# Transposing q on VectorE in 32x32 blocks instead of on TensorE, in a linear-attention and SwiGLU kernel

## The chip, the cores and the metric

The kernel runs on one core of a Trainium2 chip. A core has five engines with a queue of instructions each: TensorE (PE: matrix products out of SBUF into PSUM), VectorE (DVE), ScalarE (ACT), GpSimd (POOL) and SyncE (SP), which in this kernel issues nearly all DMAs. [...] The metric is the time of one execution on the device in microseconds, as a median over several runs.

## The reference

Linear attention without softmax, a norm for each head, and a gated feed-forward layer on the result. Everything is float32.

```python
# q, k, v: (8 batches, 8 heads, 576 tokens, 64)
kv  = np.einsum('bhsd,bhse->bhde', k, v)             # 64x64 per head and batch
out = np.einsum('bhsd,bhde->bhse', q, kv)
rms = np.sqrt(np.mean(out * out, axis=-1, keepdims=True) + 1e-06)
x   = (out / rms * g_norm)                           # -> 4608 tokens x 512
g   = x @ w_gate                                     # 512 x 1536
y   = (g * (1 / (1 + np.exp(-g)))) * (x @ w_val)     # silu(g) * val
return y @ w_out                                     # 1536 x 512
```

## The kernel before

**Blocks.** The 4608 tokens are worked off in nine blocks (n = 0 to 8) of 512. A batch has 576 tokens, so a block begins in one batch and ends in the next; `parts` (class `Att`) says which rows of which batch a tile of 128 tokens has. In each block `Att` makes x, and `Ffn` makes the feed-forward layer in an **up** stage (x times the gate and value weights, result h) and a **down** stage (h times `w_out`). The products are in Strassen-Winograd form: seven products, P1 to P7, for a 2x2 split, twice nested in the up stage from block 2 on (class `Inner`, 12 units per block, line 580). The down stage (class `Down`, line 431) takes them in the order 1, 5, 6, 7, 2, 4, 3. The weights that the nested form needs are combinations, made once and kept in DRAM; `Stream` brings them back in 51 chunks per block through the buffers `t` (nine of them, line 659). The three products P5, P7 and P4 of the down stage need combinations of `w_out` that GpSimd makes into three of the same buffers each (`turn_t`, line 111 in the profile, "T for P5", and so on).

**Attention is woven in one block ahead.** While block n is in its up stage, k and v of block n+1 are loaded (line 223) and multiplied (`kv`, line 255) in two steps, after a third and two thirds of the stage. q of block n+1 is loaded after the second (`load_q`, line 238): 128 tokens in the partitions, all 8 heads in the columns, in pieces of 64 floats. Between up and down, `turn` transposes q on TensorE against an identity matrix (line 272, 16 transposes of 128x128 in a block), into PSUM, and ScalarE copies them into `qt` (line 274). Then, in the down stage: after P1 half 0 of q is multiplied with kv (`product`, line 292), squared (ScalarE, line 303), summed (VectorE, line 304), turned into 1/rms by three Newton steps on small tiles (`root`, lines 310 to 322), and scaled (`scale`, line 330); after P6 the scaled half is transposed on TensorE (`turn_x`, line 339), and half 1 goes the same way; after P2 its `turn_x` follows, and `sums` makes the combinations of x that the next up stage needs.

**Buffers.** `ld` has four buffers (k and v of a pair of heads take one each, q takes two), `r` has five for every intermediate of 128x2048 floats, qt among them. PSUM is split into pools: a (1), b (3), c (2), m (2).

**What sets the order.** The order of instructions on each engine isn't simply that of the program. The framework's planner plays the program through on a model: each engine takes the earliest-written instruction among those that are ready and whose buffer is free, so an instruction that is ready early can be queued ahead of ones written before it. `add_manual_dep` and `issue_after` add an order by hand. Once planned, each engine works its queue strictly in order. All loads, weights included, share SyncE's queue.

The lines that matter:

```python
                for j in range(NS):
                    nc.tensor.transpose(ps[:, j], self.q[t][:, j], ident)
                if t % 2 or self.n == 1 or self.n > DEEP:
                    nc.scalar.copy(out=self.qt[:, t], in_=ps)
...
        if nxt:
            nxt.turn()
        if n + 2 < NB:
            blocks[n + 2].load_kv((0, 1))
        ffn.down(nxt.steps() if nxt else [])
```

Of the kernel before, what the change touches and what calls it, by code (L numbers as in the profile page):

```python
# [8 lines left out]
F32 = mybir.dt.float32  # L9
# [5 lines left out]
P = 128  # L15
# [3 lines left out]
def kernel(  # L19
# [41 lines left out]
    nc = tc.nc  # L61

    B, H, S, D = q.shape
    NT, DM = out.shape
    FF = moe_w_gate.shape[1]
    T = 4
    BLK = P * T
# [3 lines left out]
    NS = DM // P  # L71
# [7 lines left out]
    def pool(name, bufs, **kw):  # L79
        return ctx.enter_context(tc.tile_pool(name=name, bufs=bufs, **kw))  # L80

    consts = pool("consts", 1)
    ld_pool = pool("ld", 4)
# [30 lines left out]
    def ring():  # L114

        return r_pool.tile([P, 4, BLK], F32, name="r")
# [67 lines left out]
    class Att:  # L184
# [29 lines left out]
        def load_kv(self, js):  # L214
            if self.n == B:
                return
            for j in js:
                hs = slice(2 * j, 2 * j + 2)
                for i, (tiles, src) in enumerate(((self.k, k), (self.v, v))):
# [6 lines left out]
                        )  # L226
                    tiles.append(t.rearrange("p h (t d) -> p h t d", t=KT))

        def load_q(self, i):
            if self.n == 1:  # L230
                tiles = [t_tile().rearrange("p a b -> p (a b)") for _ in range(2)]
            else:
                ld = ld_pool.tile([P, 2 * BLK], F32, name="ld")
                tiles = [ld[:, 0:BLK], ld[:, BLK : 2 * BLK]]
            for t in range(2):
                tile_ = tiles[t].rearrange("p (h d) -> p h d", h=H)
                for b, s0, p0, p1 in self.parts(2 * i + t):
                    nc.sync.dma_start(
                        out=tile_[p0:p1], in_=q[b, :, s0 : s0 + p1 - p0, :].rearrange("h p d -> p h d")
                    )  # L240
                self.q.append(tile_.rearrange("p (j u) d -> p j (u d)", u=2))
# [22 lines left out]
        def turn_q(self, i, pools=None):  # L264

            if i == 0:
                self.qt = ring().rearrange("p t (j c) -> p t j c", j=NS)
            for t in (2 * i, 2 * i + 1):
                pool = pools[t % 2] if pools else m_psum
                ps = pool.tile([P, NS, P], F32, name=pool.name[0])  # L270
# [4 lines that stand above are left out]
                else:  # L275
                    nc.vector.tensor_copy(out=self.qt[:, t], in_=ps)
# [67 lines left out]
        def sums(self):  # L344
# [5 lines left out]
            sub(nc.vector, s4, a12, a21)  # L350
            if self.n >= DEEP:
                self.xi = x_pool.tile([P, 3, 7, P], F32, name="xi")
# [53 lines left out]
    XI = {5: 0, 7: 1, 3: 2}  # L406

    DEEP = 2

    class Quad:  # L410

# [41 lines left out]
    class Up(Quad):  # L453
# [41 lines left out]
        def multiply(self, p):  # L495
            super().multiply(p)
            ffn = self.ffn
            if ffn.n != DEEP - 1:
                return
# [136 lines left out]
    class Stream:  # L636
# [10 lines left out]
        def enable(self, n):  # L647
            if DEEP <= n < NB:
                self.next += [(n, d, c) for d in range(NP // 2) for c in range(len(CHUNKS))]
                self.pump()  # L650
# [23 lines left out]
    def t_tile(key=None):  # L674

        stream.held.append(key)
        return t_pool.tile([P, 2, 2 * P], F32, name="t")
# [128 lines left out]
    class Ffn:  # L806
# [22 lines left out]
        def up(self, fill):  # L829
# [3 lines left out]
            for d in range(NP // 2):  # L833
                if self.n < DEEP:
                    units += [Up(self, 2 * d), Up(self, 2 * d + 1)]
# [17 lines left out]
                if unit is None:  # L853
                    last.multiply(p)

        def down(self, fill):
            down = self.down_
            fill = dict(zip((1, 6, 2), fill))
            for p in (1, 5, 6, 7, 2, 4, 3):
                if p == 1:  # L860
                    down.turn_t(7, self.ended)
                if p == 6:
                    down.turn_t(4)
                down.multiply(p)
                self.make(12)
                if p in fill:
                    fill[p]()
                if p == 1:
                    down.turn_s3()
# [31 lines left out]
    def weights(upto):  # L901
        nonlocal loaded, rounded
        while rounded < min(upto, len(pieces)):
            while loaded < min(rounded + 4, len(pieces)):
                load_w(*pieces[loaded])
                loaded += 1
            round_w(*pieces[rounded])
            rounded += 1

    def t2(place, b22, b11):  # L910

        sub(nc.vector, place, b22, place)
        add(nc.vector, place, place, b11)

    blocks = [Att(n) for n in range(NB)]
# [7 lines left out]
    for n in range(NB):  # L923
        ffn = Ffn(n, blocks[n])
        nxt = blocks[n + 1] if n + 1 < NB else None
        if n == 0:

            with tc.issue_after(scaled.ins):
                weights(2)
            ffn.plain_up(0, (0,))  # L930
            scaled = blocks[0].second()
            for f in range(NF):
                with tc.issue_after(scaled.ins):
                    weights(2 * (f + 2))
                if f == 1:
                    ffn.plain_up(1, (0,))
                    ffn.plain_up(0, (1,))
                ffn.plain_up(f, (1,)) if f == 1 else ffn.plain_up(f) if f else None
            weights(len(pieces))
            pairs = wo.rearrange("p (j e) d -> p e j d", e=2)  # L940
            t2(pairs[:, 0, :, HD:DM], pairs[:, 1, :, HD:DM], pairs[:, 0, :, 0:HD])
            nxt.room = x_pool.tile([P, 3, 7, P], F32, name="xi").rearrange("p a b c -> p (a b c)")
            nxt.load_kv(range(NS))
            for i in range(2):
                nxt.load_q(i)
            ffn.plain_end()
            nxt.kv(range(NS))
        else:

            def third():  # L950
                nxt.kv((0, 1))
                nxt.load_kv((2, 3))

            def two_thirds():
                nxt.kv((2, 3))
                for i in range(2):
                    nxt.load_q(i)

            ffn.up({4: third, 8: two_thirds} if nxt else {})
        if nxt:  # L960
            nxt.turn()
        if n + 2 < NB:
            blocks[n + 2].load_kv((0, 1))
        ffn.down(nxt.steps() if nxt else [])
        if n == 0:

            with tc.issue_after(nxt.halves[0].ins):
                for j in range(NP):
                    t2(wv[j][:, 0:2], wv[j][:, 2:4], wg[j][:, 0:2])
# [31 lines left out]
```

## Time and profile before

| | |
|---|---|
| time, median of 3 runs | 1065.49 us (1065.43 to 1066.24) |
| span of the profiled execution | 1063.9 us |
| TensorE busy | 1036.4 us, 97% |
| VectorE, ScalarE, GpSimd busy | 701.6, 245.0, 365.9 us |
| granted TensorE clock | 0.988 of full speed on average, 1.00 in blocks 3 to 8 |
| DMA | 161.87 MB, 50.4% of the DMA engines' span |
| start of the down stage of blocks 3 to 7 | 473.41, 585.17, 696.93, 808.69, 917.43 us |

The rows of the profile begin with the line of the kernel, the engine and the operation, then what is written and what is read. In rows of a timeline the start and the length come first, in us; square brackets give the time for which the engine sat idle before it, and what ended that. Rows of the chain of waits give start, length and the work that then set the time. The row over a stretch gives, after its limits and length, the busy time of PE, PE's weight loads, DVE, ACT and POOL with the number of instructions, the granted clock, the share of the DMA engines and GB/s. The blocks from 2 to 7 repeat with a period of 111.76 us (block 7 is shorter since block 8 begins no new batch, and so has no k and v of its own).

### The profile page before, as it was taken

The page shows a single profiled execution, that of the slowest core. Times are in us where ns is not written, and L with a number is a line of the kernel's source. Part 1 is how long each engine was busy: PE and PEld are TensorE (multiplying, and loading weights), DVE is VectorE, ACT ScalarE, POOL GpSimd, SP SyncE. Part 2 cuts the span into 40 slices and gives each one's busy share as a digit, 9 for nine tenths or more (in the row PEclk, how much of TensorE's full clock was granted, in tenths as well). Part 3 has the DMA queues.
Part 4 walks back from the last instruction along what each step waited for, and adds up shares of the span by engine and source line. Part 5 has one row for each costly group of instructions (what it writes and reads, how often), then busy time and mean ns, then how long its engine had stood idle before and what let it go on. Part 6 is the DMA issues. An engine that isn't in the chain of part 4 may idle for free.

```text
span 1063.9 us, 21805 instructions
## 1 busy us (share of the span) xinstructions
PE 1036.4 (97%) x8780; PEld 934.8 (88%) x8780; DVE 701.6 (66%) x1245; ACT 245.0 (23%) x392; POOL 365.9 (34%) x280
## 2 busy tenths in 40 slices
PE   4899999988999999999999999999999999999998
PEld 4644688877899989998999899989999899989997
DVE  2999596778656765576666666666567566765661
ACT  2665111221221211222112211221112221211210
POOL 0000453344025701462156305640456026602670
PEclk8899999998999999999999999999999999999999
DMA  8787103565569326741576237713783265125611
GB/s 235 225 272 224 59 4 107 166 169 159 166 208 254 99 72 193 237 150 61 163 241 174 82 127 226 226 53 129 215 236 77 80 205 194 53 81 188 199 36 40
DMA packets 154644, 161.87 MB, mean 152 GB/s; under 512 B 48432, under 2 KB 105648, under 8 KB 154544
## 3 DMA queue, kind: packets, MB, share of 16 engines
q1 hardware_dynamic: 154480, 160.48, 50.4%
q8 instruction: 70, 1.15, 0.5%
q14 instruction: 30, 0.25, 0.1%
q0 software_dynamic: 64, 0.00, 0.0%
HBM read 138.02 MB, written 22.41 MB: 151 GB/s over the span
## 4 chain that ended last, share of the span: by engine, by line
PE 93%; DVE 3%; SPq 2%; DMA 1%; POOL 1%; issue 0%; ACT 0%; DVEq 0%; POOLq 0%
PE b L580 25%; PE b L431 20%; PE c L580 12%; PE c L431 10%; PE a L580 6%; PE a L431 5%; PE b L882 4%; PE c L882 4%; PE m L255 2%; PE m L339 2%; PE m L292 1%; SPq L223 1%; PE b L292 1%; DMA ld<-in_moe_w_gate_dram 1%; PE b L272 1%; PE m L272 1%
## 5 line engine op out<-in xcount | busy, mean ns | idle before, releaser
L110 POOL TENSOR_TENSOR r<-r 128x256 f32<-128x256 f32 (+1 forms) x105 | 110.3, 1056 | 363.0 <-DVE r L110 357.8
L110 DVE TENSOR_TENSOR r<-b,r 128x512 f32<-128x512 f32 (+1 forms) x273 | 162.2, 607 | 61.3 <-PE b L580 56.6
L110 DVE TENSOR_TENSOR r<-c,r 128x512 f32<-128x512 f32 (+1 forms) x179 | 109.1, 620 | 99.0 <-PE c L580 56.0
L111 POOL TENSOR_TENSOR t<-wo 128x512 f32<-128x512 f32 x81 | 112.7, 1417 | 164.7 <-DVE wo L110 109.0
L580 PE MATMUL b<-x,t 128*128 128x128 f32 x1092 | 151.2, 276 | 0.0
L580 PEld LDWEIGHTS b<-x,t 128*128 128x128 f32 x1092 | 136.0, 192 | 0.6
L110 DVE TENSOR_TENSOR r<-a,r 128x512 f32<-128x512 f32 (+1 forms) x99 | 62.6, 632 | 83.2 <-PE a L580 53.1
L112 POOL TENSOR_TENSOR h<-r 128x1024 f32<-128x1024 f32 (+1 forms) x40 | 81.5, 2054 | 93.2 <-DVE r L110 79.7
L580 PE MATMUL c<-xi,t 128*128 128x128 f32 x840 | 112.1, 275 | 0.0
L580 PEld LDWEIGHTS c<-xi,t 128*128 128x128 f32 x840 | 102.8, 192 | 0.0
L431 PE MATMUL b<-t,h 128*128 128x256 f32 x432 | 97.1, 381 | 0.0
L431 PE MATMUL b<-wo,h 128*128 128x256 f32 x432 | 96.2, 379 | 0.0
L431 PEld LDWEIGHTS b<-wo,h 128*128 128x128 f32 x432 | 81.4, 190 | 10.7
L431 PEld LDWEIGHTS b<-t,h 128*128 128x128 f32 x432 | 80.7, 190 | 11.1 <-issue 0.2
L594 ACT COPY r<-b 128x512 f32<-128x512 f32 x63 | 36.9, 586 | 219.1 <-PE b L580 191.7
L580 PE MATMUL b<-xi,t 128*128 128x128 f32 x588 | 79.7, 276 | 0.0
L580 PEld LDWEIGHTS b<-xi,t 128*128 128x128 f32 x588 | 72.4, 192 | 0.0
L580 PE MATMUL b<-x,wg 128*128 128x128 f32 x336 | 53.0, 280 | 0.0
L580 PE MATMUL b<-x,wv 128*128 128x128 f32 x336 | 51.2, 275 | 0.0
L431 PE MATMUL c<-t,s 128*128 128x256 f32 x216 | 48.9, 383 | 0.0
L431 PE MATMUL a<-wo,h 128*128 128x256 f32 x216 | 48.3, 379 | 0.0
L431 PE MATMUL c<-wo,h 128*128 128x256 f32 x216 | 48.1, 379 | 0.0
(129 smaller groups left out, 1646.2 us busy)
## 6 DMA issues: line engine op xcount, KB each, us to landing
t<-w SPq DMA_DIRECT2D x336, 256.0 KB, 2.9
out_dram<-r SPq DMA_DIRECT2D x17, 512.0 KB, 2.9
ld<-in_q_dram SPq DMA_DIRECT2D x29, 256.0 KB, 4.6
ld<-in_moe_w_gate_dram SPq DMA_DIRECT2D x12, 512.0 KB, 5.2
ld<-in_moe_w_val_dram SPq DMA_DIRECT2D x12, 512.0 KB, 5.2
ld<-in_moe_w_out_dram SPq DMA_DIRECT2D x12, 512.0 KB, 4.5
w<-t SPq DMA_DIRECT2D x36, 128.0 KB, 2.1
ld<-in_k_dram SPq DMA_DIRECT2D x26, 160.0 KB, 3.1
```

The source lines that it names most:

```text
L110: add = lambda e, o, a, b: e.tensor_tensor(out=o, in0=a, in1=b, op=OP.add)
L111: sub = lambda e, o, a, b: e.tensor_tensor(out=o, in0=a, in1=b, op=OP.subtract)
L112: mul = lambda e, o, a, b: e.tensor_tensor(out=o, in0=a, in1=b, op=OP.mult)
L223: nc.sync.dma_start(out=t[r * D : (r + 1) * D, :, 0 : m * D], in_=src[self.n, hs, s0 : s0 + m * D].rearrange("h (p t) d -> p h (t d)", t=m),)
L255: nc.tensor.matmul(self.kv_ps[r][u * D : (u + 1) * D, j, :], lhsT=self.k[j][rows, u, c, :], rhs=self.v[j][rows, u, c, :], start=(c == 0), ...
L272: nc.tensor.transpose(ps[:, j], self.q[t][:, j], ident)
L292: nc.tensor.matmul(self.ps[i][u][p : p + D, t, j, :], lhsT=self.qt[rows, 2 * i + t, j, p : p + D], rhs=kvs[b % 3][rows, j, :], start=True, ...
L339: nc.tensor.transpose(ps[:, e, t], xt[:, t, j + e], ident)
L431: nc.tensor.matmul(banks[e][:, e], lhsT=lhsT, rhs=rhs, start=first and i == 0 and (e == 0 or banks[0] is not banks[1]), stop=i == self.ste ...
L580: nc.tensor.matmul(ps[:, i, f], lhsT=self.weight(o, p, f), rhs=self.operand(o, p), start=first and (i, f) == (0, 0), stop=True, skip_group ...
L594: nc.scalar.copy(out=dst, in_=ps)
L882: nc.tensor.matmul(t, lhsT=w[f // 2][:, i, P * (f % 2) : P * (f % 2 + 1)], rhs=x[:, i, of], start=(i == 0), stop=(i == NS - 1),)
```

## The change

For the blocks from 4 on (`TURNED`), q is no longer transposed on TensorE. VectorE has a transpose within 32x32 blocks only. To make the whole transpose out of it, the load puts each 32-column quarter of a pair of heads (two heads of 64 columns) into its own 32 partitions, with the tokens in groups of 32 along the columns (`load_quarters`); transposing the 32x32 blocks in place then gives columns in the partitions and tokens along the free dimension, which is what `product` needs. A load of q is thus split into 16 DMAs for four heads (8 where all tokens are of one batch), with pieces of 32 floats, and one VectorE instruction of 128x1024 turns four heads. `qt` is laid out by pair of heads and then by token tile, so that the output of the transpose is contiguous.

So that the loads are there in time, q of block n+2 is loaded at the start of the down stage of block n, a whole block earlier; to keep within the four `ld` buffers, k and v go in four steps of one pair each, after units 2, 5, 8 and 11 of the up stage, each followed by the load of the next pair. T for P4 on GpSimd is made to wait for the scaling of half 0.

```diff
+        def load_quarters(self, i):
+            ld = ld_pool.tile([P, 2 * BLK], F32, name="ld")
+            to = ld.rearrange("p (j g d) -> p j g d", j=2, d=P // 4)
+            cut = 2 * self.n
+            spans = [(self.n - 1, S - D * self.n, 0, cut), (self.n, 0, cut, BLK // 32)]
+            for j in range(2):
+                for r in range(4):
+                    h, d = divmod(r, 2)
+                    for b, s0, g0, g1 in spans:
+                        if g1 > g0:
+                            nc.sync.dma_start(
+                                out=to[32 * r : 32 * (r + 1), j, g0:g1],
+                                in_=q[b, 4 * i + 2 * j + h, s0 : s0 + 32 * (g1 - g0), 32 * d : 32 * (d + 1)].rearrange(
+                                    "(g p) d -> p g d", p=32
+                                ),
+                            )
+            self.q.append(ld)
...
             if i == 0:
-                self.qt = ring().rearrange("p t (j c) -> p t j c", j=NS)
+                self.qt = ring().rearrange("p j (t c) -> p t j c", t=T)
+            if self.n >= TURNED:
+                to = self.qt[:, :, 2 * i : 2 * i + 2].rearrange("p t j c -> p j t c")
+                nc.vector.transpose(out=to.rearrange("p j t c -> p (j t c)"), in_=self.q[i])
+                return
...
                 if p == 6:
-                    down.turn_t(4)
+                    down.turn_t(4, nxt.halves[0] if nxt and nxt.n >= TURNED else None)
...
-            ffn.up({4: third, 8: two_thirds} if nxt else {})
+            def pair(j):
+                nxt.kv((j,))
+                if j + 1 < NS:
+                    nxt.load_kv((j + 1,))
+
+            if not nxt:
+                steps = {}
+            elif n + 1 < TURNED:
+                steps = {4: third, 8: two_thirds}
+            else:
+                steps = {3 * j + 2: lambda j=j: pair(j) for j in range(NS)}
+            ffn.up(steps)
         if nxt:
             nxt.turn()
         if n + 2 < NB:
-            blocks[n + 2].load_kv((0, 1))
-        ffn.down(nxt.steps() if nxt else [])
+            if n + 2 < TURNED:
+                blocks[n + 2].load_kv((0, 1))
+            else:
+                blocks[n + 2].load_kv((0,))
+                for i in range(2):
+                    blocks[n + 2].load_q(i)
+        ffn.down(nxt)
```

More of the change, by code (lines that the diff above doesn't have):

```diff
@@ L227, in load_kv @@
                     tiles.append(t.rearrange("p h (t d) -> p h t d", t=KT))
+        def load_quarters(self, i):
[15 more added lines that the diff above has]
+            self.q.append(ld)
         def load_q(self, i):
+            if self.n >= TURNED:
+                self.load_quarters(i)
+                return
             if self.n == 1:
@@ L266, in turn_q @@
             if i == 0:
-                self.qt = ring().rearrange("p t (j c) -> p t j c", j=NS)
+                self.qt = ring().rearrange("p j (t c) -> p t j c", t=T)
+            if self.n >= TURNED:
+                to = self.qt[:, :, 2 * i : 2 * i + 2].rearrange("p t j c -> p j t c")
+                nc.vector.transpose(out=to.rearrange("p j t c -> p (j t c)"), in_=self.q[i])
+                return
             for t in (2 * i, 2 * i + 1):
@@ L408 @@
     DEEP = 2
+    TURNED = 4
     class Quad:
@@ L854, in up, with down @@
                     last.multiply(p)
-        def down(self, fill):
+        def down(self, nxt):
             down = self.down_
-            fill = dict(zip((1, 6, 2), fill))
+            fill = dict(zip((1, 6, 2), nxt.steps() if nxt else ()))
             for p in (1, 5, 6, 7, 2, 4, 3):
```

## Prediction

> **What bounds the kernel now.** I read the page's busy table first, then the busy time over one block of tokens, then the chain of waits across the end of that block's up stage, and last VectorE's and SyncE's own order of time there. The first two show what the time is made of: TensorE is busy for 97% of the whole span and for all 111.80 us of the block from 473.2 to 585.0 us, at the full granted clock (the 1.00 behind the counts), while VectorE has 40 us to spare, ScalarE 89 us, and the DMA engines half their time. The waits listed for TensorE between 360 and 1020 us are none.
>
> ```profile
> PE 1036.4 (97%) x8780; PEld 934.8 (88%) x8780; DVE 701.6 (66%) x1245; ACT 245.0 (23%) x392; POOL 365.9 (34%) x280
> ...
> 473.20:585.00 111.80, 111.80 (x1062) 106.25 (x1061) 71.45 (x121) 22.69 (x36) 42.67 (x32) 1.00 0.53 157
> ```
>
> The chain of waits from 580 to 590 us runs on TensorE alone: start, length, engine, tile, line. Line 272, the transposes of q, is four pieces in it, between the last product of the up stage (line 580) and P1 of the down stage (line 431).
>
> ```profile
> 582.38 1.05 PE b L580 x8
> 583.42 0.44 PE m L272 x4
> 583.86 0.44 PE b L272 x4
> 584.30 0.44 PE m L272 x4
> 584.74 0.44 PE b L272 x4
> 585.17 5.18 PE b L431 x24
> ```
>
> VectorE in the same stretch: what must be watched is what it does from 583.5 us on, and the three instructions of 16 columns (the first is shown) that take 1.2 us where their likes take 0.17 us.
>
> ```profile
> 583.52 0.69 DVE L110 TENSOR_TENSOR r<-b,r 128x512 f32<-128x512 f32 x1 [0.41 <-PE b L580]
> 584.31 1.23 DVE L112 TENSOR_TENSOR h<-r 128x1024 f32<-128x1024 f32 x1
> ...
> 587.94 0.69 DVE L111 TENSOR_TENSOR h<-s,h 128x512 f32<-128x512 f32 x1
> 590.39 2.49 DVE L111 TENSOR_TENSOR h<-h 128x1536 f32<-128x1536 f32 x1 [1.76 <-PE b L431]
> 592.80 1.26 DVE L304 TENSOR_REDUCE z<-r 128x8 f32<-128x512 f32 x2
> 594.10 1.17 DVE L310 TENSOR_SCALAR z<-z 128x16 f32<-128x16 f32 x1
> ...
> 597.75 0.17 DVE L321 TENSOR_TENSOR a<-a,z 128x16 f32<-128x16 f32 x1
> ...
> 600.10 0.68 DVE L112 TENSOR_TENSOR r<-a,y 128x512 f32<-128x512 f32 x1
> ```
>
> SyncE, which issues every load: after the last weights of this block's up stage (574.37 us) it has little to do for 19 us, and the weights of the next block (line 659) then come slowly, because their buffers are given up by P5, P7 and P4.
>
> ```profile
> 574.37 0.33 SPq L659 DMA_DIRECT2D t<-w  x1
> 574.74 1.24 SPq L223 DMA_DIRECT2D ld<-in_v_dram  x2
> 584.33 1.25 SPq L223 DMA_DIRECT2D ld<-in_k_dram  x2
> 585.67 1.25 SPq L223 DMA_DIRECT2D ld<-in_v_dram  x2
> 593.44 26.25 SPq L659 DMA_DIRECT2D t<-w  x8
> ```
>
> **What the Trainium skill says.** "VectorE: DVE Perf Modes", section "The three transpose paths": VectorE transposes 32x32 blocks only, 311 ns for 128x128 bf16. "Vector Engine (DVE) Microarchitecture Reference", section 3.8: one element per cycle and lane. No row of this trace has such an instruction. "SBUF — State Buffer", section "Who interferes with whom": VectorE and GpSimd share one pair of ports, an exclusive lock, and the second to come waits for the whole instruction of the first. The trace agrees: GpSimd runs six subtractions (line 111, T for P7 and P4) from 588.77 to 597.69 us, and the slow small instructions above end exactly there. "DMA: Bandwidth & Descriptors", Specifications: pieces under 512 B are under line rate. Here the 256-byte pieces of q fill the DMA engines (share 1.00) at 242 GB/s in 559.5 to 563.2 us, where other stretches move 238 GB/s at a share of 0.76: a mild penalty.
>
> **The change part by part.**
> 1. The transposes on TensorE go, for blocks 4 to 8. From the chain: 583.42 to 585.17 us is 1.75 us, with no wait in it, and nothing else of TensorE's depends on its length. P1 needs its first h at once and the last pair only after two thirds of itself, 583.42 + 3.5 = 586.9 us; VectorE finished that one at 585.54. P5 needs the sums that end at 588.63; P1 will end at 583.42 + 5.18 = 588.60, the product takes 1.1 us more, so P5 finds them done. Five blocks by 1.75 us: **8.75 us** off the path.
> 2. The four evictions on ScalarE (line 274, 0.59 us each) go: worth nothing, ScalarE is 80% idle.
> 3. Two transposes on VectorE per block, 128x1024 each. Estimate from the skill: 311 ns less 128 cycles at 0.96 GHz (133 ns) leaves 0.18 us fixed, and 1024 cycles are 1.07 us: 1.25 us. The nearest row, a 128x1024 multiplication, took 1.23 us. I take 1.25; the upper end, should 4-byte data go at half rate, is 2.3 us. Two are 2.5 us (4.6 at most) on an engine with 40 us idle per block. They depend on loads that now come a whole block earlier, so the planner, which orders by readiness, can place them in an idle stretch well before the product; the half-microsecond sums of the up stage that they then delay have slack, since a bank is written again only one or two products (0.9 us each) later. Price on the path 0 to 1.0 us per block (two transposes, each holding one eviction up by its length less that slack of some 0.75 us); I take 0.1.
> 4. The loads of q: 32 instead of 4 or 5 DMAs per block (16 for block 8), 128-byte instead of 256-byte pieces. SyncE's row for line 238 has a median of 593 ns per DMA: 32 by 0.6 = 19.2 us, against 3.6 us. They are queued behind the transposes that free the buffers, so they fall into the thin stretch of SyncE from 574 on; the next up stage starts at 626.21 - 1.75 = 624.5 us. Counting there the q loads, 2.5 us of k and v, nine weight loads by 0.33 and a store, some 27 of 50 us are taken. The DMA engines: 1 MB in 19 us is 55 GB/s, in a stage with shares of 0.2 to 0.35. Cost zero, hidden behind the down stage.
> 5. k and v by single pairs at steps 2, 5, 8 and 11 of 12 instead of two by two. Same products: twice 1.31 us in the chain. Two more switches between shapes; where the 64x64 shape begins in the product at 590.35 us, the chain gives its first matmul 0.20 us and the next ones 0.01 to 0.04. I take 0.1 per block, 0 to 0.35. Each pair has three steps, some 18 us, to load where DMAs land in 3 us.
> 6. T for P4 waits for the norm of half 0. Behind it on GpSimd stands nothing until 637 us. It takes the lock off most of the chain squares, sums, root, scale. That chain ended at 600.78, and turn_x of half 0 starts at 602.00: 1.2 us to spare. With TensorE 1.75 us earlier turn_x wants it by 600.25, so without this edit the lock, whose end does not move, would cost about half a microsecond. With it: P7's three subtractions still run from 588.7 to about 593; the sums end near 592.4, the root's eleven instructions take about 2.3 us and the scaling 1.3, so scale ends near 597. T for P4 then runs to about 601; P4 starts at 615.85 - 1.75 = 614.1. Cost zero.
>
> Sum: 8.75 - 5 x 0.2 = 7.75 us: 1065.49 - 7.75 = **1057.7 us**.
>
> **Rivals.**
> A, half given back: the transposes sit between evictions at the end of up and TensorE waits at several banks, or at the upper price of 2.3 us. Parts 3 and 5 at their upper ends sum to 1.0 + 0.35 = 1.35 per block, so 1063.5; in the middle (0.7) 1060.2 us. For: VectorE's idle gaps in up are mostly 0.2 us. Against: it has gaps of 2 to 3.5 us beside the products of k and v (535.4 to 538.9 us).
> B, slower: a wait replaces the removed work. If the transposes run behind the sums of h (588.63 + 2.5 = 591.1 us), the product, wanted at 588.60, waits 2.5 us: 0.75 us lost per block, 1069.2 us. Or a q load costs SyncE over 1.0 us, so that 32 of them from 591 us end near 623 and the first weights of the next block land 3 us into its up stage: 4 by 3 us less 8.75, again near 1069. For: one in-order queue for all loads. Against: rows of 0.6 us, and TensorE can take P5 before the product.
> C, no change: losses of some 1.75 us per block cancel the gain, 1065.5 us. It needs a coincidence.
>
> **Chances.** Forecast 0.60, A 0.22, B 0.13, C 0.05. So faster 0.82, same 0.05, slower 0.13. The range starts at 1056.0 (all 8.75 us, less 0.7 us that the runs scatter) and reaches over A's upper end to 1064.5; B and C stay outside.
>
> **What would show it.** Right: TensorE still without waits from 360 us on, line 272 gone after 360 us, a block period of 111.76 - 1.55 = 110.2 us, the small instructions of line 310 to 322 at 0.17 us except for those beside P7's T, transposes of about 1.25 us. Wrong: waits of TensorE at the product for VectorE, at line 580 for weights or for banks, or SyncE still busy with q when the next up stage starts.

## The result and the profile after

The changed kernel takes 1059.15 us (median of six runs, 1058.09 to 1060.62) against 1065.51 us for the kernel before in the same session (1064.58 to 1066.26). The ratio is 0.994, with a 95% interval of 0.9927 to 0.9953: a gain of 6.4 us (5.0 to 7.8). Forecast were 1057.7 us and a gain of 7.75 us. The interval does not quite exclude that gain; the period of a block, 110.70 us where 110.2 was forecast (111.76 before), does.

First the busy table and the row of one block, now 110.70 us long:

```profile
PE 1032.9 (98%) x8700; PEld 928.2 (88%) x8700; DVE 701.7 (66%) x1255; ACT 234.9 (22%) x372; POOL 367.5 (35%) x280
...
479.30:590.00 110.70, 110.70 (x1047) 104.58 (x1045) 71.92 (x123) 20.60 (x31) 42.99 (x33) 1.00 0.55 159
```

TensorE is as full as before: 110.70 busy us in a stretch of 110.70 us, and no wait is listed for it from 360 to 1020 us. TensorE's matmuls fell by 80, which is five blocks of 16 transposes. ScalarE lost the 20 evictions (392 to 372 instructions) and 10 us. VectorE gained ten instructions, the ten transposes.

The end of the up stage in the chain of waits (start, length, engine, tile, line; line 609 was line 580 before, 460 was 431):

```profile
581.51 0.89 PE b L609 x8
582.40 0.22 PE c L609 x2
582.62 1.30 PE b L460 x6
583.92 0.89 PE b L609 x8
584.81 4.11 PE b L460 x18
```

The four pieces of q are gone from it. Something else has changed place, which the forecast did not have: six matmuls of P1 (line 460) now stand ahead of the last product of the up stage (line 609 at 583.92 us).

These rows also hold two pauses that are too short for the list of waits. The last product of the up stage took 1.05 us before; its eight matmuls take 0.89 now, so a pause of 0.16 us is gone. And the last 18 matmuls of P1 take 4.11 us, where at the pace of the 24 of before (5.18 us) they would take 3.89: a new pause of 0.22 us. In the single records of the trace it lies before the last eight of them, at 586.9 us, where VectorE has just ended the first of the two multiplications that make h and begin at 585.64 us in the next rows.

VectorE over the same time (start, length, then line, operation and tiles):

```profile
577.97 1.23 DVE L293 STREAM_TRANSPOSE r<-ld 128x1024 f32<-128x1024 f32 x1
...
581.56 1.22 DVE L293 STREAM_TRANSPOSE r<-ld 128x1024 f32<-128x1024 f32 x1
...
584.92 0.69 DVE L110 TENSOR_TENSOR r<-b,r 128x512 f32<-128x512 f32 x1 [0.96 <-PE b L609]
585.64 2.39 DVE L112 TENSOR_TENSOR h<-r 128x1024 f32<-128x1024 f32 x2
...
592.57 1.17 DVE L337 TENSOR_SCALAR z<-z 128x16 f32<-128x16 f32 x1
593.77 1.19 DVE L340 TENSOR_SCALAR y<-z 128x16 int32<-128x16 int32 x1
594.99 0.17 DVE L347 SCALAR_TENSOR_TENSOR a<-y 128x16 f32<-128x16 f32 x1
...
597.55 0.68 DVE L112 TENSOR_TENSOR r<-a,y 128x512 f32<-128x512 f32 x1
```

Three things are to be seen. The transposes take 1.23 us, and they stand in the last 7 us of the up stage, among the sums of the last products, not in an idle stretch earlier. Of the small instructions only two still take 1.2 us; they fall beside GpSimd's T for P7, and T for P4 has moved behind the norm:

```profile
589.62 5.31 POOL L111 TENSOR_TENSOR t<-wo 128x512 f32<-128x512 f32 x3 [6.66 <-DVE h L111]
598.31 3.72 POOL L111 TENSOR_TENSOR t<-wo 128x512 f32<-128x512 f32 x3 [3.38 <-DVE r L112]
```

SyncE in the down stage (start, length and number of DMAs in a row):

```profile
579.23 17.77 SPq L241 DMA_DIRECT2D ld<-in_q_dram  x32
597.10 22.88 SPq L688 DMA_DIRECT2D t<-w  x9
```

The 32 loads of q take 17.77 us, 0.555 us each, and fill a stretch that was nearly empty. The weights of the next block (line 688) start right after, at 597.10 us, and are spread over 22.88 us (26.25 for eight of them before) by the buffers that P5, P7 and P4 give up.

**Where the time went.** The starts of P5 in the chain of waits in us, from block 2, the last that the change leaves as it was, to block 8. "Gained" is by how much the distance from the start above has become shorter than before; the two columns on the right are of the best kernel of the experiments:

| P5 of block | before | after | gained | best kernel | gained |
|---|---|---|---|---|---|
| 2 | 367.93 | 368.55 | | 366.08 | |
| 3 | 479.69 | 479.31 | 1.00 | 476.23 | 1.61 |
| 4 | 591.45 | 590.01 | 1.06 | 586.32 | 1.67 |
| 5 | 703.20 | 700.71 | 1.05 | 696.41 | 1.66 |
| 6 | 814.96 | 811.41 | 1.06 | 806.51 | 1.66 |
| 7 | 923.71 | 918.49 | 1.67 | 913.59 | 1.67 |
| 8 | 1029.62 | 1024.34 | 0.06 | 1019.44 | 0.06 |

The transposes of TensorE were worth 1.75 us. Block 7, which makes no k and v products, keeps 1.67 of it. Blocks 3 to 6 keep 1.00 to 1.06: another 0.61 us or so is lost in each block that multiplies k and v. What lies ahead of the table scatters: P5 of block 1 began at 255.51 and at 256.79 us in two profiles of the same changed kernel, so times are compared here by periods inside a profile, and whole times only by their intervals.

### The profile page after: what moved, and what is told of

Its sections match the earlier page's. It is cut to its first block, busy times and chain, and to the rows that moved or that the text cites. A ratio compares the mean times of both kernels' runs of the same rounds, so it can differ in the third digit from the quotient of the medians.

```text
span 1058.9 us, 21788 instructions
## 1 busy us (share of the span) xinstructions
PE 1032.9 (98%) x8700; PEld 928.2 (88%) x8700; DVE 701.7 (66%) x1255; ACT 234.9 (22%) x372; POOL 367.5 (35%) x280
## 4 chain that ended last, share of the span: by engine, by line
PE 92%; DVE 3%; DMA 2%; SPq 2%; POOL 1%; issue 0%; ACT 0%; DVEq 0%; POOLq 0%; ACTq 0%
PE b L609 25%; PE b L460 20%; PE c L609 12%; PE c L460 10%; PE a L609 6%; PE a L460 5%; PE c L912 4%; PE b L912 4%; PE m L278 2%; PE m L366 1%; PE m L319 1%; SPq L223 1%; PE b L319 1%; DMA ld<-in_moe_w_gate_dram 1%; DVE r L111 1%; DVE r L110 1%
```

## The experiments

Each ran beside the kernel before on the same chip. A period is the time from a product of one block to the same product of the next, in blocks that multiply k and v.

**The change again, as the yardstick for the others.** No edit.

> The changed kernel once more, as the yardstick for the three beside it. Every theory: 6 to 7 us below the kernel before, so 1058.8 to 1059.5 us; down stages of blocks 3 to 6 (their P5) 110.70 us apart.

Measured: 1059.52 us against 1065.28, ratio 0.9944 (0.9932 to 0.9957), period 110.70 us.

**Only the four pieces of k and v, put into the kernel before.** q stays on TensorE and its loads stay late; k and v are still loaded two pairs at a time.

```diff
-            ffn.up({4: third, 8: two_thirds} if nxt else {})
+            # for n + 1 >= 4; load_q stands at the end of the last
+            steps = {2: lambda: nxt.kv((0,)), 4: second, 6: lambda: nxt.kv((2,)), 8: fourth}
+            ffn.up(steps)
```

> The kernel before with the products of k and v alone cut from two pieces per block into four (one pair of heads at units 2, 4, 6 and 8), for blocks 4 to 7; loads, q and T for P4 as before. Theory 1 (each piece of 64x64 products costs TensorE some 0.28 us of switching between shapes, which is what ate most of the 2.4 us that the change fell short of 8.75): two more pieces in four blocks, 8 x 0.28 = 2.2 us slower than before, 1067.7 us; period of blocks 3 to 6 from 111.76 to about 112.3 us. Rival 1 (the switches cost 0.1 us per block as the prediction had it, and the loss sits in the tail of the up stage, where the planner moved part of P1 ahead of P4): 1065.5 to 1066 us, period 111.8 us.

Measured: 1067.6 us, ratio 1.0023 (1.0014 to 1.0033), slower by 2.3 us. The period is 112.44 against 111.76 us: 0.68 us in each of four blocks, 2.7 us. The chain shows where. First the kernel before, around its second piece of k and v (line 255, two pairs; the chain lists 70 of the 72 matmuls):

```profile
534.70 1.31 PE m L255 x70
536.01 1.09 PE b L580 x8
```

and the experiment, one pair:

```profile
536.35 0.73 PE m L255 x36
537.08 1.09 PE b L580 x8
```

Half of the work costs 0.73 us, not the half of 1.31, 0.655; and the product after it takes 1.09 us where its like takes 0.89. Both surcharges come with every piece: some 0.15 us in front (2 x 0.73 less 1.31) and 0.20 us behind, so 0.35 us for each of the two extra pieces, 0.70 us in a block. That is the measured loss. The changed kernel has the same rows (0.73 us at 541.44, and 1.09 us for the product behind it).

The difference of this experiment's period to that of the change, 112.44 less 110.70, is 1.74 us, and it is also the first part of the forecast measured almost by itself: with k and v in four pieces on both sides, the change is worth 1.74 us in a block, where the chain had given the transposes 1.75.

**The change with k and v in two pieces.** To have room for q early and for two pairs at a time, the four buffers of `ld` are split into two for q and two larger ones, each of which holds k and v of one pair. In block 0 the loads of weights take the two kinds in turn.

```diff
-    ld_pool = pool("ld", 4)
+    ld_pool = pool("ld", 2)
+    kv_pool = pool("lkv", 2)     # k and v of one pair in one tile
...
-                steps = {3 * j + 2: lambda j=j: pair(j) for j in range(NS)}
+                steps = {4: third, 8: late}     # late: nxt.kv((2, 3))
...
-                blocks[n + 2].load_kv((0,))
+                blocks[n + 2].load_kv((0, 1))
```

> The changed kernel with k and v back in two pieces per block (pairs 0 and 1 after unit 4, pairs 2 and 3 after unit 8) and q loaded early all the same. For this the four load buffers are split into two of 1024 and two of 1280 columns, the second kind holding k and v of one pair together; loads of weights in block 0 take the two kinds in turn. Theory 1 (switching): 2.2 to 2.4 us faster than the changed kernel, about 1056.8 us, period of blocks 3 to 6 about 110.1 us. Rival 1 (tail of the up stage): as the changed kernel, 1059 us, period 110.7 us.

Measured: 1059.64 us, ratio 0.9946 (0.9934 to 0.9959), no faster than the change. But the period is 110.10 us, as the theory of the switches says; the gain was spent earlier. P1 of block 2 starts at 364.87 us, against 361.00 in the profile of the yardstick: 3.9 us lost in the blocks that were not to change. With the buffers of q free from the start, the planner had moved the loads of q of block 2 forward and set VectorE's work in block 1 in another order. So the run is two effects in one, and it needed a repair before it could count.

**The same with that side effect taken out.** The loads of q of block 2 keep the place that the program gives them.

```diff
+                    if self.n == 2:
+                        tc.keep_in_program_order(dma)
```

> The changed kernel with k and v in two pieces and the split load buffers, as tried before, but with the loads of q of block 2 held in the written order on SyncE's queue, so that VectorE's order in block 1 is that of the changed kernel again. If the 2.4 us gained in blocks 3 to 6 (period 110.10 instead of 110.70 us) were lost in block 1 through the planner's other order there: 1056.7 to 1057.5 us, period 110.1 us, and block 1 as long as in the changed kernel. Rival: block 1 is longer for another cause of the split buffers, 1059.5 us.

Measured: 1057.33 us against 1064.54, ratio 0.9932 (0.9919 to 0.9945), period 110.09 us. The chain around its second piece of k and v has the rows of the kernel before again (here from the second profile of this kernel, that of the last experiment):

```profile
531.19 1.31 PE m L288 x70
532.50 1.09 PE b L619 x8
```

The period differs from that of the change by 110.70 - 110.09 = 0.61 us, the same 0.61 us that the table above shows between block 7 and the blocks before it. In the up stage only the number and the places of the pieces differ, and the buffers that k and v are loaded into. That the loss here is 0.61 us, and not 0.68 as in the experiment above, fits the pause in P1: in this kernel it is 0.29 us, in the change 0.22.

**T for P4 set free again in the change.**

```diff
-                    down.turn_t(4, nxt.halves[0] if nxt and nxt.n >= TURNED else None)
+                    down.turn_t(4)
```

> The changed kernel without the wait of T for P4 on the norm of half 0. Prediction's part 6 (the shared ports then slow the root until about 598 us in the terms of the block at 585, turn_x of half 0 wants the scaled half by 600.6): the chain ends within 0.5 us of the need, so 0 to 0.5 us lost per block, 1059 to 1061.6 us; three or four instructions of lines 337 to 349 at 1.2 us instead of two. Rival 2 (the wait is worth nothing because the chain has over 2 us of slack in the changed kernel, 598.2 against 600.6): 1059 us, and no wait of TensorE before line 366. Rival 3 (it is worth more, over 1 us per block): above 1064 us.

Measured: 1064.01 us, ratio 0.9989 (0.9981 to 0.9998); the period is 111.65 us, so 0.95 us more in each block, and 4.5 of the 5.8 us that the change gained beside it are gone. GpSimd runs six subtractions in one go:

```profile
699.69 8.98 POOL L111 TENSOR_TENSOR t<-wo 128x512 f32<-128x512 f32 x6 [6.67 <-DVE h L111]
```

VectorE beside it:

```profile
702.64 1.17 DVE L337 TENSOR_SCALAR z<-z 128x16 f32<-128x16 f32 x1
...
707.52 1.19 DVE L349 SCALAR_TENSOR_TENSOR y<-a,y 128x16 f32<-128x16 f32 x1
708.74 0.18 DVE L347 SCALAR_TENSOR_TENSOR a<-y 128x16 f32<-128x16 f32 x1
...
710.67 0.68 DVE L112 TENSOR_TENSOR r<-a,y 128x512 f32<-128x512 f32 x1
```

Five instructions in a row (the first and the last of them are shown) that need 0.17 us take 1.17 to 1.19 us each, and the sixth, after GpSimd's end at 708.67, 0.18. The scaling ends at 711.35, and turn_x, the transposes of x on TensorE, waits for it:

```profile
PE m L366 <- DVE r L112: 3.8, 5, 0.8
```

Five waits, one per block, 0.8 us at the longest, 3.8 us in all (five times 0.95 is 4.75; the trace puts the rest down to no wait). So most of the gain hangs on the one edit that has nothing to do with q.

**T for P4 behind the norm in the kernel before**, as the counterpart.

```diff
-                    down.turn_t(4)
+                    down.turn_t(4, nxt.halves[0] if nxt and nxt.n >= 4 else None)
```

> The kernel before with the wait of T for P4 on the norm of half 0 alone, for blocks 4 to 8. Theory 5 (the lock matters only once TensorE is early; in the kernel before turn_x of half 0 starts 1.2 us after the norm ends): no change, 1064.5 to 1066 us, period 111.76 us, and the norm of half 0 ends some 3 us earlier. Rival (the freed ports are worth something by themselves): 1063 us or less.

Measured: 1064.43 us against 1065.18, ratio 0.9998 (0.9989 to 1.0006): no change, and the period is 111.76 us as before. The norm of the block at 697 us ends at 708.16 us, where it ended at 712.19 us before, four microseconds earlier, and nothing waited for it. The edit buys slack that only a faster TensorE uses up.

**The transposes on VectorE twice**, to ask how much room there is for them.

```diff
                 nc.vector.transpose(out=to.rearrange("p j t c -> p (j t c)"), in_=self.q[i])
+                nc.vector.transpose(out=to.rearrange("p j t c -> p (j t c)"), in_=self.q[i])
```

> The changed kernel with every transpose on VectorE done twice in a row (same input and output), so 20 instead of 10 of 1.23 us. Theory 3 (the planner puts them into the last 6 us of the up stage, where VectorE is the engine that hands h to P1, and P1 waits for h there already by 0.2 to 0.4 us): the added 2.46 us per block come out almost whole as waits of P1, 5 x 1.2 to 2.4 us, so 1065 to 1071 us. Rival 4 (hidden, as the prediction's part 3 priced it: at most what exceeds the slack of one eviction): 1059.5 to 1061 us.

Measured: 1061.46 us against 1064.54, ratio 0.9969 (0.9956 to 0.9981); the period is 111.17 us. For 2.46 us more of VectorE the block lost 0.47 us: more than nothing, and less than was expected if VectorE set the time there throughout. The time lies just above the range of rival 4. TensorE now has a wait that the list shows, five times, before the last matmuls of P1 (line 461 here):

```profile
PE b L461 <- DVE h L112: 0.9, 5, 0.2
```

In the chain of this kernel lines 293 and 294 are the transposes:

```profile
576.22 0.91 PE c L610 x8
...
577.16 0.99 DVE r L293
578.15 0.97 DVE r L110 x3
...
584.63 1.15 DVE r L294
585.78 1.12 DVE h L112
...
586.94 1.99 PE b L461 x8
```

From 577.16 to 586.94 us the chain runs over VectorE, where in the changed kernel it stays on TensorE. VectorE has 39 us idle in the whole block (110.70 less 71.92), but little where the transposes stand. In the change it begins to make h (row of 585.64 us) 1.88 us after the last product of the up stage starts on TensorE (583.76 us in the timeline), here 2.99 us after it (585.70 and 582.71): h comes 1.11 us later, so only 1.35 of the added 2.46 us fell into idle time. That TensorE lost no more than 0.47 us goes with a second move of the planner: two thirds of the product of q with kv (42 of its 64 matmuls, line 320) now stand ahead of the last eight matmuls of P1, and fill most of the time until h is there.

**The loads of q where they were**: the change with q loaded after two thirds of the up stage, for use at its end.

```diff
-                steps = {3 * j + 2: lambda j=j: pair(j) for j in range(NS)}
+                steps = {4: third, 8: two_thirds}     # two_thirds ends with load_q
...
-                blocks[n + 2].load_kv((0,))
-                for i in range(2):
-                    blocks[n + 2].load_q(i)
+                blocks[n + 2].load_kv((0, 1))
```

> The changed kernel with the loads where the kernel before has them: k and v in two pieces, q of the next block after two thirds of the up stage, but in quarters and transposed on VectorE. Theory 4 (SyncE's queue: 32 loads of q by 0.55 us are 17.8 us during which no weights are issued, the nine buffers hold some 12 us of weights, a load lands in 3 us): TensorE waits for weights some 8 us in each of blocks 3 to 6, 1065 to 1090 us, with waits of line 609 for DMA. Rival 5 (the planner and the nine buffers cover it): 2.4 us faster than the changed kernel for the two pieces of k and v, 1057 us.

Measured: 1091.86 us, ratio 1.0258 (1.0241 to 1.0275): 27 us slower than before and 32 us slower than the change, with periods of 118 to 119 us. SyncE's queue in the up stage:

```profile
564.52 17.52 SPq L241 DMA_DIRECT2D ld<-in_q_dram  x32
582.14 6.17 SPq L688 DMA_DIRECT2D t<-w  x10
```

For 17.52 us no weights are issued, and TensorE stands for them at line 609, in four blocks, for 6.0 us on average:

```profile
PE b L609 <- DMA t<-w: 23.9, 4, 6.7
```

This is rival B's second mechanism, made real by the place of the loads: the same 32 DMAs make TensorE wait for nothing at 579 us, and for up to 6.7 us in a block at 564 us.

**The best kernel with VectorE's transposes from block 3 on.**

```diff
-TURNED = 4
+TURNED = 3
```

> As the kernel with two pieces and the held loads of q, with block 3 turned on VectorE too (TURNED = 3). If a turned block is worth 1.75 us less 0.1 wherever it is: 1.65 us faster than that kernel, about 1055.3 us. Rival: the early q of block 3 and the other order in block 1 cost as much: 1057 us or more.

Measured: 1058.53 us, ratio 0.9945 (0.9931 to 0.996). This is slower than the same kernel with the change from block 4 on (1057.33 us beside it), as the rival had it. The transposes of q of block 3 would gain between P5 of block 1 and P5 of block 2, but that distance is now 114.51 us (254.17 to 368.68), where the best kernel has 111.76 (254.32 to 366.08). The 32 loads now stand in block 1's down stage ahead of a store of the weight combinations (line 750) that the weights of block 2 are read from:

```profile
252.18 17.05 SPq L249 DMA_DIRECT2D ld<-in_q_dram  x32
269.33 0.56 SPq L750 DMA_DIRECT2D w<-t  x1
...
289.82 4.65 SPq L698 DMA_DIRECT2D t<-w  x9
```

In the best kernel, with the change from block 4, the same store goes at 252.15 us and the weights follow from 274.37 us.

So the stretch is 2.75 us longer, although 1.75 us of transposes are gone from it. That the loads ahead of the store are the cause is read from these rows; no run moved the store alone.

**The change and the best kernel side by side once more.**

> The changed kernel on the same chip as the version beside it: 1058.5 to 1059.5 us.

> The version with k and v in two pieces and held loads of q, beside the changed kernel: 2.4 us below it by the period (110.08 instead of 110.70 us in four blocks), 1056.5 to 1057 us; a rival in which the early blocks take back a part gives 0.5 to 1.5 us.

Measured: the change 1059.36 us, ratio 0.9949 (0.9935 to 0.9962); the change with k and v in two pieces 1055.43 us (1055.13 to 1056.1), ratio 0.9917 (0.9903 to 0.993), against 1065.18 us before. It beats both kernels, and by more than was expected. Its block:

```profile
477.00:587.00 110.00, 109.98 (x1045) 104.20 (x1044) 71.63 (x123) 20.60 (x32) 42.69 (x33) 1.00 0.56 160
```

TensorE is still full; only less is in it. Around the last product of its up stage (line 619 here) P1 (line 470) stops as in the change:

```profile
580.16 0.89 PE b L619 x8
581.05 2.16 PE b L470 x10
583.22 0.02 issue
583.24 1.99 PE b L470 x8
```

Ten matmuls keep the pace of before; the last eight end 4.18 us after the product does, where 18 at that pace need 3.89: a stop of 0.29 us.

Of the kernel's lead over the change in this pair, 3.9 us, the periods explain 4 x 0.61 = 2.4 us; the rest lies ahead of block 3 and is no gain that the runs show: P5 of block 2 begins at 367.10 and at 366.08 us in the two profiles of this very kernel, and at 367.27 to 368.60 in three of the change.

## Why the prediction came out as it did

The mechanism was right in the main: TensorE sets the time, and work taken off it is gained. One term of the sum was wrong in size, the pieces of k and v, and it took the period to 110.70 us, not to the 110.2 that the prediction named as a sign of being right. The forecast gain of 7.75 us was 1.4 too high.

From P5 of block 2 to P5 of block 8 the table gives a gain of 5.90 us. It divides into 8.75 for the transposes, less 4 x 0.61 = 2.4 for the pieces of k and v, less 5 x 0.08 = 0.4 at the end of up (1.75 less the 1.67 us that block 7 and the best kernel keep). The 0.61 and 0.08 are read from the same table, so this is no check of it; what checks it from outside is the experiment on the pieces alone, with 0.68 us a block. The other 0.5 of the 6.4 us lies ahead of P5 of block 2, where profiles of one kernel differ by more than that. So it is in part luck that the whole time came so near.

1. **Transposes off TensorE, 8.75 us.** Right: 1.74 us per block by the periods 112.44 and 110.70, 1.67 by 111.76 and 110.09.
2. **Evictions for nothing.** Nothing contradicts it: ScalarE is busy 20.60 us in a block. It was not tried alone.
3. **VectorE's transposes.** The length was right, 1.23 us against an estimate of 1.25 from the Trainium skill's "VectorE: DVE Perf Modes", section "The three transpose paths", and the one element per cycle of its "Vector Engine (DVE) Microarchitecture Reference", section 3.8. The net price was near too, 0.08 against 0.1 us, but that was luck, since the reason given for it failed. The transposes are not placed "in an idle stretch well before the product" but among the last sums of the up stage. There six matmuls of P1 moved ahead of the last product, and the prediction's 1.4 us between h (585.54) and the matmuls that need it (586.9) are gone with them: TensorE stops for h for 0.22 us in blocks 3 to 6. The rows put no name to so short a stop; in the run with doubled transposes, where it is longer, the list names h. Block 7 and the best kernel have 0.29 us. Against this stands the pause of 0.16 us before the transposes that is no longer there, which the prediction did not have either: 1.75 + 0.16 - 0.29 = 1.62 us of the 1.67 that the best kernel gains in a block. That the transposes made the planner move the six matmuls, by holding up the sums that free a bank for the last product, is likely but not shown; why it puts them no earlier is open. They write `qt`, which needs one of five `r` buffers; that none is free sooner is argued, not tried.
4. **The loads of q.** Right: 17.77 us against 19.2, hidden. With them back in their old place the kernel is 32 us slower than the change, so the new place is not a convenience but a condition.
5. **k and v in four pieces: the failed term.** "I take 0.1 per block, 0 to 0.35"; it is 0.61, above the upper end. The forecast saw the first 64x64 matmul's 0.20 us and counted it for one edge of a piece. The same chain held the other half: the product behind a piece takes 1.09 us, where others of eight matmuls take 0.89. Each piece has two edges, 0.15 and 0.20 us, and two pieces were added. The Trainium skill says in "TensorEngine Tiling (Array Packing)", section "Key Properties", that a change of the tiling mode drains TensorE; it gives no figure. The trace fits this, with 0.35 us for the way there and back; it shows the two surcharges, not the draining. Read for a piece between two products, the page's sentence means both edges. With 0.61 in place of 0.1 in four blocks (the forecast counted five, but block 7 has none) and 0.08 in five, the sum is 5.9 instead of 7.75.
6. **T for P4.** Right in kind: the lock is off the chain, the norm ends at 598.23 (forecast 597), T for P4 runs to 602.03 (forecast 601). Without the edit "about half a microsecond" was said; it is 0.95. The forecast let GpSimd end where it had ended, 1.75 us later only as seen from TensorE. But GpSimd waits for h from VectorE (line 111), and VectorE makes it only after the last product of the up stage, for which it sits idle 0.96 us in the changed kernel (row of 584.92 us). That product now ends 5.20 us ahead of P5 (584.81 and 590.01), before it was 8.03 us (583.42 and 591.45), because the transposes are gone from between and six matmuls of P1 have moved ahead of it. So T for P7 starts 0.39 us ahead of P5 (589.62), before it was 2.68 us (588.77), 2.29 us later. The Trainium skill's "SBUF — State Buffer", section "Who interferes with whom", has the lock; that each of a chain of short instructions pays for a whole one of the other engine is what the rows add.

The rivals: A's middle (0.7 us lost per block, 1060.2 us) is close to what a block loses in fact, 0.69, but by the pieces of k and v and not by the evictions it named; its sum had five such blocks, and there are four. B's two waits, of the product for its transposes and of the next up stage for its weights, did not occur in the change. One of them, SyncE's queue, appeared at once when the loads were put back.

## What to carry to other kernels

Where one engine is full, count what a change adds to that engine as carefully as what it removes: here work of 1.75 us was taken away and 0.61 us put back by cutting another product into more pieces. Price a change of matmul shape from both of its edges in the chain, the first matmul of the new shape and the first product after it. And ask of spare time where it lies: VectorE had 39 us in a block but little more than 1 us where the work landed, SyncE had 19 us in the down stage and no room for them in the up stage.

## What the runs showed of the hardware

- A piece of 64x64 matmuls between products of 128x128 (float32) costs 0.35 us beyond its own work: 0.15 us in front, 0.20 us behind. By the periods, with two pieces more in a block, it is 0.31 to 0.34 us for each.
- VectorE transposes 128x1024 float32 in 32x32 blocks in 1.221 to 1.236 us, as forecast (1.25), and not at the upper price of 2.3 us.
- Beside a GpSimd instruction on SBUF, VectorE's instructions of 16 columns took 1.17 to 1.19 us where alone they take 0.17: five in a row cost 5 us.
- A load of q in pieces of 128 bytes takes SyncE 0.555 us to issue and lands 2.0 us after it (median). In the down stage 32 of them moved 1 MB in 18 us without a wait of TensorE; in the up stage they cost it up to 6.7 us.
